# Attention's calls recorded and issued in one written order for all engines

## The chip, the cores and the metric

The kernel runs on one core of one Trainium2 chip. What is measured is the device time of one execution in microseconds (us). A core has five engines that each work off a list of their own: PE (matrix products and transposes), DVE and ACT (element-wise work and exponentials), POOL (element-wise work) and SP, which here only issues transfers. The lists meet at semaphores: an instruction waits until those that it needs have signalled.

## What is computed

Three stages follow each other. The first is causal attention with a decay over 32 heads (4 batches of 8), 576 positions and 64 columns a head:

```python
scores = scale * np.matmul(q, k.transpose(0, 1, 3, 2))
cum = np.cumsum(log_f, axis=-1)
decay = cum[:, :, :, None] - cum[:, :, None, :]
scores = np.where(causal, -1000000000.0, scores + decay)
scores = scores - np.max(scores, axis=-1, keepdims=True)
attn = np.exp(scores)
attn = attn / (np.sum(attn, axis=-1, keepdims=True) + 1e-09)
return np.matmul(attn, v).astype(np.float32)
```

Its result, 4 x 576 x 512, goes through the second stage: the real part of a Fourier transform over positions and columns is added, rows are normalized, and a layer 512 -> 2048 -> 512 with a ReLU is added. The third stage forms `x*cos(theta)` and `x*sin(theta)`, mixes positions with two 576 x 576 matrices, and adds a layer of 512 x 512.

## The kernel before, in words

Attention and the Fourier transforms of the first three batches are written in `phase1`. Heads go in 16 pairs (pair p has heads 2p and 2p+1); four pairs make a batch. A loop runs over heads, n from -1 to 32. In one turn it interleaves, step by step, the work of several heads, each written as a generator:

- `prep_units`: for head n+2, ACT casts the raw queries and keys to `hi` and `q` (L222, L224), and POOL forms the low parts, in `hi` and `kl` (L226, L228; DVE has one of them for head 0).
- `score_units`: for head n+1, five row blocks of 576, 448, 320, 192 and 66 columns. Each is two products, L247 (`hi` with `hi`) and L248 (`kl` with `q`), into a PSUM bank `pa` out of three. DVE adds the mask, takes the row minimum `mn` and writes `P` (L256); ACT exponentiates `P` in place, with row sums (L261). The block of 576 columns comes in two parts, 448 and 128. At the end of a pair ACT and DVE form `rz`, the reciprocal of the sums, and POOL spreads it to `wide` (L267).
- `turn_units`: for head n, the blocks of `P` are transposed (L286) into four banks `pb` out of three buffers, and copied to `PT` (L289), three by DVE, the fourth by ACT.
- `av_units`: for the pair before, 14 value products (L321) of `PT` with `v` into the bank `pt`, in 64-column halves of the two heads; then `spread` transposes `wide` (L300), one block into `pa`, four into `pb`, and ACT copies both to `R` (L301, 128 and 448 columns).
- `evac_pair`: DVE multiplies `pt` by `R` to `X` or `Y` (L347). For every second pair a few rows of `Y` are moved by transfers that SP issues (L356 to L363), and POOL forms `E` = X+Y and `O` = X-Y (L367, L370).
- `fft_units`: after four pairs, one batch's transform: POOL has `ee`, `oo` and the low parts `el`, `ol`, ACT `eh`, `oh`, PE the products L428, L439 and L451, and DVE and POOL what lies between (`yl`, `zl`, `ea`, `oa`, `u`).

Each engine's list is put together by a scheduler that goes by priorities: score products have 20 more than the rest, value products 100 more. In `av_units` the first value product also depends, by hand, on all eight copies to `PT` of its pair (the reason is named "one run"), so that none of the 14 comes before them. Phases 2 and 3 (normalization, layers, decoding of the 64-bit weights by DVE and ACT) stand behind; their work begins to be mixed in from turn n = 31 on, and the normalization of batch 0 from turn 29 on.

## Time and profile before

| | us |
|---|---|
| median of 3 runs | 939.33 |
| lowest and highest run | 938.42, 941.68 |
| profiled execution, its own time | 940.95 |
| its span in the trace | 939.2 |
| first matmul of attention starts | 9.44 |
| last block of value products starts | 249.42 |

The rows further below come from one profiled execution. A time is in us from the start of the span; a line number such as L321 is that of the code above. PE's matmuls overlap, since the engine takes the next before the last has left it: a busy PE is not a PE at its peak. PEld is PE's loading of weights (the stationary matrix), which goes beside its products. PEclk is the clock that PE was granted, as a share of the full one. A row that ends in `[0.36 <-DVE PT L289]` says that the engine stood idle for 0.36 us ahead of it, until DVE's instruction of L289 on tile `PT` had finished. An fp32 product has two records, so a block of 14 shows as x28.

### The profile page before, as it was taken

How to read it: one execution, taken by the hardware profiler on the slowest of the kernel's cores; microseconds unless marked ns; L12 is line 12 of the kernel's file. 1: busy time of each engine (PE TensorE's matmuls, PEld its weight loads, DVE VectorE, ACT ScalarE, POOL GpSimd, SP SyncE). 2: the span in 40 equal slices, each digit the busy share in tenths (PEclk: the TensorE clock that was granted, in tenths of full speed). 3: DMA queues.
4: the chain of work that ended last, by engine and by line, in shares of the span. 5: the costliest groups of instructions: out<-in, count | busy, mean ns of one | idle time of the engine just before them, and what ended most of it. 6: DMA issues, size and time to landing. Idle time of an engine off the chain costs nothing.

```text
span 939.2 us, 15860 instructions
## 1 busy us (share of the span) xinstructions
PE 894.1 (95%) x5960; PEld 841.5 (90%) x5960; DVE 606.7 (65%) x1495; ACT 417.8 (44%) x1014; POOL 326.3 (35%) x369
## 2 busy tenths in 40 slices
PE   4998999989788999999999999999999999999998
PEld 3777878777577999999999999999999999999998
DVE  8676676674899943456654565536687756747563
ACT  6888678685544332222221232223235534434331
POOL 6676788676601343000000000000035635425330
PEclk9999999999979999999999999999999999999999
DMA  5643423231233300013322122514310000010001
GB/s 167 202 149 106 130 93 114 83 105 40 82 97 93 90 1 1 1 46 90 91 91 90 45 90 74 199 29 127 109 51 2 1 26 27 14 40 1 26 27 51
DMA packets 23725, 68.04 MB, mean 72 GB/s; under 512 B 2906, under 2 KB 6362, under 8 KB 23648
## 3 DMA queue, kind: packets, MB, share of 16 engines
q1 hardware_dynamic: 20608, 62.88, 21.2%
q0 software_dynamic: 2320, 2.97, 1.2%
q10 hardware_dynamic: 720, 1.18, 0.4%
q8 instruction: 47, 0.77, 0.3%
q14 instruction: 30, 0.25, 0.1%
HBM read 57.91 MB, written 9.07 MB: 71 GB/s over the span
## 4 chain that ended last, share of the span: by engine, by line
PE 62%; DVE 5%; ACT 1%; issue 1%; DMA 0%; POOL 0%; DVEq 0%; SPq 0%; ACTq 0%
PE pa L767 19%; PE pb L781 11%; PE po L781 8%; PE pb L988 7%; PE pa L999 5%; PE pa L952 5%; PE po L988 5%; PE pa L948 1%; DVE u L789 1%; DVE kra L959 1%; DVE a L587 0%; DVE a L585 0%; DVE uc L754 0%; DVE kra L962 0%; PE pb L952 0%
## 5 line engine op out<-in xcount | busy, mean ns | idle before, releaser
L767 PE MATMUL pa<-un,wf 128*128 128x384 f32 x1152 | 221.4, 342 | 6.3 <-ACT un L755 3.4
L767 PEld LDWEIGHTS pa<-un,wf 128*128 128x128 f32 x1152 | 204.6, 191 | 10.2 <-DVE un L756 4.5
L773 DVE SCALAR_TENSOR_TENSOR h<-pa,h 128x384 fp32r<-128x384 f32 x96 | 52.4, 555 | 139.0 <-ACT h L772 139.0
L781 PE MATMUL pb<-h,wf 128*128 128x384 f32 x660 | 134.2, 337 | 0.3 <-DVE u L789 0.3
L781 PEld LDWEIGHTS pb<-h,wf 128*128 128x128 f32 x660 | 116.0, 188 | 1.1 <-DVE u L789 0.6
L781 PE MATMUL po<-h,wf 128*128 128x384 f32 x492 | 105.2, 340 | 0.4 <-ACT h L772 0.2
L772 ACT ACTIVATE h<-pa 128x384 fp32r<-128x384 f32 x96 | 45.7, 489 | 132.7 <-PE pa L767 130.0
L261 ACT ACTIVATE P<-P,mn 128x448 f32<-128x448 f32 (+4 forms) x160 | 89.0, 558 | 33.6 <-DVE mn L256 33.4
L988 PE MATMUL pb<-wtk,z 128*128 128x288 f32 x513 | 98.3, 295 | 1.3 <-ACT z L977 1.3
L944 POOL COPY xd<-u 128x64 f32<-128x64 f32 x32 | 6.9, 255 | 264.5 <-DVE u L789 254.5
L256 DVE CUSTOM_DVE_ANT_0 P<-pa,mask 128x448 f32<-128x448 f32 (+3 forms) x160 | 69.4, 457 | 42.1 <-PE pa L248 35.6
L781 PEld LDWEIGHTS po<-h,wf 128*128 128x128 f32 x492 | 86.2, 188 | 3.6 <-ACT h L772 1.9
L978 POOL TENSOR_TENSOR z<-kra,z 128x256 fp32r<-128x256 f32 x72 | 53.1, 752 | 93.5 <-ACT z L977 93.4
L247 PE MATMUL pa<-hi 128*128 128x448 f32 (+1 forms) x192 | 65.8, 364 | 20.5 <-DVE hi L226 9.4
L988 PEld LDWEIGHTS pb<-wtk,z 128*128 128x128 f32 x513 | 79.3, 188 | 2.0 <-ACT z L977 2.0
L988 PE MATMUL po<-wtk,z 128*128 128x288 f32 x351 | 75.2, 295 | 0.8 <-ACT z L977 0.8
L286 PE MATMUL pb<-ident,P 128*128 128x128 f32 (+2 forms) x480 | 73.9, 284 | 1.7 <-DVE uc L724 0.9
L247 PEld LDWEIGHTS pa<-hi 128*128 128x128 f32 x192 | 38.2, 204 | 30.1 <-issue 14.5
L289 DVE COPY PT<-pb 128x448 f32<-128x448 f32 (+1 forms) x96 | 55.6, 594 | 14.2 <-PE pb L286 13.3
L952 PE MATMUL pa<-wf,xs 128*128 128x256 f32 x456 | 64.1, 289 | 0.0
L286 PEld LDWEIGHTS pb<-ident,P 128*128 128x128 f32 (+2 forms) x480 | 56.6, 147 | 7.5 <-ACT P L261 1.2
L248 PE MATMUL pa<-kl,q 66*128 66x448 f32 (+1 forms) x192 | 58.0, 337 | 1.4 <-POOL kl L228 0.7
(206 smaller groups left out, 1667.0 us busy)
## 6 DMA issues: line engine op xcount, KB each, us to landing
raw<-in_qk SPq DMA_DIRECT2D x31, 576.0 KB
raw<-in_wf SPq DMA_DIRECT2D x32, 512.0 KB
raw<-in_wtk SPq DMA_DIRECT2D x18, 288.0 KB
v<-in_vp SPq DMA_DIRECT2D x16, 320.0 KB
out<-ob SPq DMA_DIRECT2D x12, 288.0 KB
dft<-in_dft POOLq DMA_DIRECT2D x8, 346.0 KB, 5.4
raw<-in_wth SPq DMA_DIRECT2D x4, 512.0 KB
st_wth<-raw SPq DMA_DIRECT2D x4, 512.0 KB
```

What stands on the lines that cost most here:

```text
L247: nc.tensor.matmul(t[:, 0 : b - a], hi[:, 1, q], hi[:, 0, a:b], start=True, stop=False)
L248: nc.tensor.matmul(t[:, 0 : b - a], q2[:, q], kl[:, g, a:b], start=False, stop=True)
L256: nc.vector.tensor_tensor_reduce(out=p[:, a:b], in0=t[:, 0 : b - a], in1=self.mask[:, m0 + a : m0 + b], scale=-0.125, scalar=least, op0=AL ...
L261: nc.scalar.activation(p, p, AF.Exp, bias=lowest, scale=-1.0, accum_out=zs[:, g, i : i + 1])
L286: nc.tensor.transpose(ps[:, o : o + n], src, self.ident[0:n, 0:n])
L289: copy = nc.scalar.copy(dst, ps[:, d : d + w]) if bank > 2 else nc.vector.tensor_copy(dst, ps[:, d : d + w])
L767: nc.tensor.matmul(ps[:, 0:CH], t[:, l, 128 * d : 128 * d + 128], un[r][:, d], start=n == 0, stop=n == 11)
L773: nc.vector.scalar_tensor_tensor(h[:, 1], ps[:, 0:CH], 0.0, f(h[:, 0]), ALU.max, ALU.subtract)
L781: nc.tensor.matmul(outs[d], t[:, l, 128 * d : 128 * d + 128], h[:, r], start=k % G == 0 and n == 0, stop=k % G == G - 1 and n == 2,)
L952: nc.tensor.matmul(th, xs[:, l, d], self.wth[d][:, r, 256 * hf : 256 * hf + 256], start=n == 0, stop=n == 11)
L978: nc.gpsimd.tensor_tensor(z[:, 1], t, f(z[:, 0]), ALU.subtract)
L988: nc.tensor.matmul(acc[k][th], z[:, l, 128 * k : 128 * k + 128], self.wtk[kt][:, r, 288 * th : 288 * th + 288], start=first and i == 0 and ...
```

## The change

Calls that `phase1` makes on the engines until turn n = 31 are no longer issued where they are written. `Recorder` takes the place of `nc` and keeps them in a list; early in turn n = 31 `emit` issues them, in the order that `order(0, n)` decodes from a table of digits. Each character of the table says which of the calls not yet issued comes next. They go out under `manual_schedule`, so that the order of issue is the order on every engine, and the buffers of PSUM follow each other in that order. What is written behind that point (the transposes of head 31, pair 15, phases 2 and 3) is scheduled as before. The dependency "one run" and the list of copies that it used are gone. Since recorded calls are issued from one place, they all bear line L71 in the lists of after.

```diff
--- before.py
+++ after.py
@@ -56,6 +56,33 @@
 
 def f(ap):
     return ap.bitcast(F32)
+
+
+class Recorder:
+    def __init__(self, nc):
+        self.nc, self.calls, self.live = nc, [], True
+
+    def __getattr__(self, name):
+        return Queue(self, name)
+
+    def emit(self, order):
+        for k in order:
+            engine, name, a, kw = self.calls[k]
+            getattr(getattr(self.nc, engine), name)(*a, **kw)
+        self.live = False
+
+
+class Queue:
+    def __init__(self, rec, engine):
+        self.rec, self.engine = rec, engine
+
+    def __getattr__(self, name):
+        def call(*a, **kw):
+            if not self.rec.live:
+                return getattr(getattr(self.rec.nc, self.engine), name)(*a, **kw)
+            self.rec.calls.append((self.engine, name, a, kw))
+
+        return call
 
 
 class Net:
@@ -274,7 +301,7 @@
         nc = self.nc
         P = hd["P"]
         PT = self.w3.tile([128, 1600], F32, tag="PT", name="PT", bufs=4)
-        hd["PT"], hd["copies"] = PT, []
+        hd["PT"] = PT
         for bank, pieces in enumerate(TURNED):
             ps = self.bank_b()
             for j, a, b, off in pieces:
@@ -286,8 +313,7 @@
                     nc.tensor.transpose(ps[:, o : o + n], src, self.ident[0:n, 0:n])
             d, w = TSKIP[bank], TWIDE[bank]
             dst = PT[:, PTOFF[bank] : PTOFF[bank] + w]
-            copy = nc.scalar.copy(dst, ps[:, d : d + w]) if bank > 2 else nc.vector.tensor_copy(dst, ps[:, d : d + w])
-            hd["copies"].append(copy)
+            (nc.scalar.copy if bank > 2 else nc.vector.tensor_copy)(dst, ps[:, d : d + w])
             yield
 
     def spread(self, p, T, wide):
@@ -310,7 +336,6 @@
             for j, a, b, off in pieces
         }
         yield
-        first = True
         with self.tc.high_priority(100):
             for j in range(5):
                 for lo_q, hi_q in ((0, SPLIT), (SPLIT, 576)):
@@ -318,21 +343,13 @@
                     if a >= hi_q:
                         continue
                     for g in (1, 0):
-                        ins = nc.tensor.matmul(
+                        nc.tensor.matmul(
                             T[64 * g : 64 * g + 64, T0 + a : T0 + hi_q],
                             v[:, j, g, :],
                             hds[g]["PT"][:, place[j, a] : place[j, a] + hi_q - a],
                             start=j == 0,
                             stop=j == 4 or (j == 1 and hi_q == SPLIT),
                         )
-                        if first:
-                            for copy in hds[0]["copies"] + hds[1]["copies"]:
-                                self.tc.add_manual_dep(
-                                    ins.ins, copy.ins.name,
-                                    mybir.DependencyInfo(mybir.DependencyClass.NoSync, mybir.DependencyReason.DATA),
-                                    reason="one run",
-                                )
-                            first = False
         for _ in range(5):
             yield
         R = self.spread(m % NP, T, wide)
@@ -478,6 +495,7 @@
     def phase1(self):
         pair, heads = self.p1_open()
         NH = B * H
+        rec = self.nc = Recorder(self.nc)
         pairs, heads, raws = {0: pair}, dict(enumerate(heads)), {}
         fft = None
         self.tick = 0
@@ -521,6 +539,9 @@
                 av = self.av_units(m, [heads[2 * m], heads[2 * m + 1]], T, pairs[m]["rz"], done)
             t = self.turn_units(heads[n]) if 0 <= n < NH else iter(())
             if n == NH - 1:
+                with self.tc.manual_schedule():
+                    rec.emit(order(0, len(rec.calls)))
+                self.nc = rec.nc
                 self.p1a.close()
                 self.p2_open()
                 self.load(0)
@@ -1099,6 +1120,47 @@
         self.pu0.close()
 
 
+DIGITS = "#$%&()*+,-./0123456789:;<=>?@ABCDEFGHIJKLMNOPQRSTUVWXYZ[]^_`abcdefghijklmnopqrstuvwxyz|"
+ORDERS = (
+    (
+        "&~$6~+X~,e~,e~,e~,e#*35=2)297*+1%)~$$).&|+%/.#$+##///#)-%+(*#)#**#$3<-=[#-811$.T5%;0..252~*p~*p.3361"
...
+    ),
+)
+
+
+def order(part, n):
+    left, taken, digits = list(range(n)), [], iter(ORDERS[part])
+    for c in digits:
+        k = DIGITS.find(c)
+        if k < 0:
+            k = DIGITS.index(next(digits)) * len(DIGITS) + DIGITS.index(next(digits))
+        taken.append(left.pop(k))
+    return taken
+
+
 def body(tc, ins, out):
     with ExitStack() as ctx:
         net = Net(ctx, tc, ins, out)
```

How instructions move shows at three places. First PE at the value products of pair 1 (heads 2 and 3; `P_107` is the buffer of head 4, whose work goes beside it). A row is a group of equal instructions, with the tile written, the tiles read, and the size. Before:

```order
L321 MATMUL pt<-PT,v 64x64 x2
L321 MATMUL pt<-PT,v 64x384 x2
L247 MATMUL pa<-hi 128x192
L248 MATMUL pa<-kl,q_100 128x192
L247 MATMUL pa<-hi 128x66
L248 MATMUL pa<-kl,q_100 128x66
L286 MATMUL pb<-ident,P_107 128x128 x2
L286 MATMUL pb<-ident,P_107 128x66
L286 MATMUL pb<-ident,P_107 128x126
L321 MATMUL pt<-PT,v 64x320 x2
L321 MATMUL pt<-PT,v 64x192 x2
L321 MATMUL pt<-PT,v 64x64 x2
```

After:

```order
L71 MATMUL pb<-ident,P_107 128x128
L71 MATMUL pt<-PT,v 64x192 x2
L71 MATMUL pt<-PT,v 64x384 x2
L71 MATMUL pt<-PT,v 64x64 x2
L71 MATMUL pt<-PT,v 64x384 x2
L71 MATMUL pt<-PT,v 64x320 x2
L71 MATMUL pt<-PT,v 64x192 x2
L71 MATMUL pt<-PT,v 64x64 x2
L71 MATMUL pa<-ident,wide 128x128
L71 MATMUL pb<-ident,P_107 128x128 x3
```

The last six of the 14 products stood behind two row blocks of scores and four transposes of head 4's third bank; now the 14 are one run, the transpose of `wide` into `pa` follows at once, and more of head 4's transposes stand behind.

Second, ACT around the same pair (`P_107` is head 4, `P_108` head 5). Before:

```order
L261 ACTIVATE P_108,zs_95<-P_108,mn 128x448
L261 ACTIVATE P_108,zs_95<-P_108,mn 128x576
L261 ACTIVATE P_108,zs_95<-P_108,mn 128x320
L222 CAST hi<-raw 128x1152
L224 CAST q_100<-raw 64x576
L261 ACTIVATE P_108,zs_95<-P_108,mn 128x192
L261 ACTIVATE P_108,zs_95<-P_108,mn 128x66
L289 COPY PT<-pb 128x320
L301 COPY R<-pa 128x128
```

After:

```order
L71 COPY PT<-pb 128x320
L71 ACTIVATE P_107,zs_95<-P_107,mn 128x448
L71 ACTIVATE P_107,zs_95<-P_107,mn 128x320
L71 CAST q_99<-raw 64x576
L71 ACTIVATE P_107,zs_95<-P_107,mn 128x192
L71 ACTIVATE P_107,zs_95<-P_107,mn 128x66
L71 COPY R<-pa 128x128
L71 ACTIVATE P_108,zs_95<-P_108,mn 128x576
L71 CAST hi<-raw 128x1152
```

The copy of 128 columns from `pa` to `R` stood behind all exponentials of head 5 and behind head 4's fourth copy to `PT`; it now stands between the last exponential of head 4 and the first of head 5, and the cast to `hi` follows directly on that first one.

Third, POOL in the third batch (`hi_2731` before and `hi_767` after are head 29; `hi_2836` and `hi_792` are head 30; `E`, `O`, `ee`, `oo`, `el` and `ol` belong to the batch's transform). Before:

```order
L391 MEMSET xx_3312 1x2
L367 TENSOR_TENSOR E_1940<-X_2358,Y_2555 128x576
L370 TENSOR_TENSOR O_1941<-X_2358,Y_2555 128x576
L226 TENSOR_TENSOR hi_2731<-raw_2596,hi_2731 64x576
L228 TENSOR_TENSOR kl_2514<-raw_2596,hi_2731 64x576
L399 TENSOR_TENSOR ee_2646<-E_1940 128x2x287
L267 TENSOR_SCALAR wide_2694<-rz1_98 128x640
L403 TENSOR_TENSOR oo_2647<-O_1941 128x2x287
L226 TENSOR_TENSOR hi_2836<-raw_2702,hi_2836 64x576
L228 TENSOR_TENSOR kl_2698<-raw_2702,hi_2836 64x576
```

After:

```order
L71 TENSOR_TENSOR hi_767<-raw_733,hi_767 64x576
L71 TENSOR_TENSOR xl_90<-xx_745,xh_89 1x290
L71 TENSOR_TENSOR kl_712<-raw_733,hi_767 64x576
L408 MEMSET xx_3315 1x2
L71 TENSOR_TENSOR E_596<-X_684,Y_725 128x576
L71 TENSOR_TENSOR ee_743<-E_596 128x2x287
L71 TENSOR_TENSOR O_597<-X_684,Y_725 128x576
L71 TENSOR_TENSOR oo_744<-O_597 128x2x287
L71 TENSOR_TENSOR el_747<-ee_743,eh_746 128x580
L71 TENSOR_TENSOR ol_749<-oo_744,oh_748 128x576
L71 TENSOR_SCALAR wide_755<-rz1_98 128x640
L71 TENSOR_TENSOR hi_792<-raw_758,hi_792 64x576
```

Head 29's `hi` and `kl` stood behind `E` and `O`; they now stand ahead of both, and `ee`, `oo`, `el` and `ol` stand ahead of `wide` and of head 30.

## Rows read from the trace of the kernel before

**Rows 1.** The chain of work that ended last, by engine, whole span

```profile
PE 62%; DVE 5%; ACT 1%; issue 1%; DMA 0%; POOL 0%; DVEq 0%; SPq 0%; ACTq 0%
```

**Rows 2.** Stretches: length, busy us of each engine (count), PEclk, DMA share, GB/s

```profile
41.00:52.00 11.00, 11.00 (x95) 9.03 (x93) 8.45 (x30) 10.50 (x30) 8.36 (x9) 1.00 0.91 267
145.70:149.20 3.50, 3.50 (x16) 3.42 (x17) 2.35 (x10) 3.17 (x14) 3.42 (x4) 0.51 0.00 0
210.00:214.00 4.00, 3.79 (x17) 1.85 (x19) 0.34 (x4) 1.94 (x7) 3.92 (x5) 0.58 0.29 81
33.00:255.00 222.00, 204.00 (x1591) 165.88 (x1589) 152.57 (x531) 165.51 (x465) 161.97 (x150) 0.98 0.34 105
255.00:320.00 65.00, 57.09 (x307) 51.39 (x308) 62.47 (x123) 28.97 (x56) 14.19 (x12) 0.84 0.32 94
```

**Rows 3.** What PE waited for, 33 to 255 us: total, times, longest

```profile
PE pa L247 <- POOL hi L226: 3.5, 2, 2.6
PE pa L247 <- DVE mn L256: 3.2, 8, 0.8
PE pt L321 <- DVE PT L289: 3.2, 5, 1.3
PE pa L247 <- ACT R L301: 1.1, 2, 0.7
...
PE pb L428 <- POOL el L406: 0.6, 2, 0.4
```

**Rows 4.** PE's timeline, value products: start, us, operation, records, idle time before

```profile
46.01 1.95 PE L321 MATMUL pt<-PT,v 128*64 128x192 f32 x16
...
48.90 1.20 PE L321 MATMUL pt<-PT,v 128*64 128x320 f32 x12
...
67.41 2.93 PE L321 MATMUL pt<-PT,v 128*64 128x192 f32 x28
...
89.74 1.95 PE L321 MATMUL pt<-PT,v 128*64 128x192 f32 x16 [1.34 <-DVE PT L289]
...
249.42 2.93 PE L321 MATMUL pt<-PT,v 128*64 128x192 f32 x28 [0.36 <-DVE PT L289]
```

**Rows 5.** POOL's timeline ahead of head 29's cast

```profile
205.89 1.42 POOL L367 TENSOR_TENSOR E<-X,Y 128x576 f32<-128x576 f32 x1 [2.15 <-DVE PT L289]
...
208.75 1.40 POOL L226 TENSOR_TENSOR hi<-raw,hi 64x576 fp32r<-64x576 f32 x1
```

**Rows 6.** PE's timeline at head 29's first score product

```profile
210.21 0.47 PE L247 MATMUL pa<-hi 128*128 128x448 f32 x1 [2.58 <-POOL hi L226]
210.60 4.59 PE L321 MATMUL pt<-PT,v 128*64 128x192 f32 x28
```

**Rows 7.** ACT's timeline in one pair without FFT work

```profile
41.93 0.67 ACT L261 ACTIVATE P<-P,mn 128x448 f32<-128x448 f32 x1
...
42.60 0.55 ACT L261 ACTIVATE P<-P,mn 128x320 f32<-128x320 f32 x1
...
43.56 0.45 ACT L261 ACTIVATE P<-P,mn 128x192 f32<-128x192 f32 x1
...
45.05 0.67 ACT L224 CAST q<-raw 64x576 fp32r<-64x576 f32 x1
45.62 0.35 ACT L261 ACTIVATE P<-P,mn 128x66 f32<-128x66 f32 x1
...
45.97 0.40 ACT L289 COPY PT<-pb 128x320 f32<-128x320 f32 x1
```

**Rows 8.** What ACT waited for, 33 to 255 us

```profile
ACT P L261 <- DVE mn L256: 27.2, 28, 2.9
ACT R L301 <- PE pb L300: 4.8, 5, 2.9
```

**Rows 9.** What POOL waited for, 33 to 255 us

```profile
POOL Y L358 <- DMA Y<-Y: 12.2, 3, 6.0
```

**Rows 10.** DVE's copies to PT at the start

```profile
22.09 1.14 DVE L289 COPY PT<-pb 128x448 f32<-128x448 f32 x2
```

23 lines of the change are left out of this document (added).

## The prediction

> **What bounds the kernel now.** The profiled execution spans 939.20 us and took 940.95 us, so 1.75 us lie around its span; the median of the runs shown is 939.33 us. Sums below are made against 940.95, and the last step takes off 1.6 us to stand against the median.
>
> I read the chain of the work that ended last first. Its shares are those of phases 2 and 3 [rows 1], which the edit does not reorder. So attention counts only through the moment at which it ends. The table by stages says the same: from 255 to 320 us DVE is busy 62.5 of 65 us [rows 2], with decoding, norm and the rest of the FFT, all issued behind the recorded part. That stretch begins when attention ends (pair 15's value products start at 249.42 us [rows 4]), so I let a microsecond won or lost before 250 us pass to the end unchanged.
>
> Between 33 and 255 us the same table shows PE busy 204 of 222 us, ACT 165.5, POOL 162, DVE 152.6: no engine is full over the whole stretch. Inside it there are two regimes. Pairs without FFT work (37 to 90 us) go by ACT: from 41 to 52 us ACT is busy 10.50 of 11 us [rows 2], and from pair 1's value products to pair 5's it is 89.74 - 46.01 = 43.7 us [rows 4], 10.9 for each of four pairs. Pairs with FFT work (90 to 240 us) go by whichever engine comes last, and there PE's table of waits has nearly all its entries [rows 3].
>
> [...] From 41 to 52 us the matmul row reads 11.00 and the weight row 9.03 [rows 2]; by the first nothing is to be won there, by the second up to 2 us in 11, some 10 us over five pairs, and the sum below would come out near 922. My sum takes nothing there because of ACT's row.
>
> **The change, part by part.** The number and kind of compute instructions stay. What changes is their order on each engine, and with it which wait comes last.
>
> *Value products in one block.* Before, 9 of 16 pairs have their 14 products in two groups (25 groups of L321 stand in PE's timeline). The two groups take 1.95 + 1.20 = 3.15 us, a whole one 2.93 [rows 4]: 0.22 us a split, 9 x 0.22 = 2.0 us. Five of the nine lie before 92 us, where ACT sets the pace, and I count them at nothing: if ACT did not cover them, they would give 1.1 us more. Four count: **-0.9**.
>
> *The wait at the block's head.* Before, PE stands 3.2 us ahead of L321 for PT's copies by DVE [rows 3]. The written order puts each recorded block behind transposes and scores of the next head, so the copy has that long to land. Pair 15's block is left with the scheduler, and it keeps its 0.36 us [rows 4]. The ends are 0 (the time reappears at the next wait) and -2.8 (all but that); I take **-2.0**, nearer to the far end since work stands in between, less part of the 1.34 us at 89.74 [rows 4], which ACT may fill.
>
> *Head 29's cast.* At 205.89 us POOL starts E after a wait of 2.15 us, then O, and only then, at 208.75, hi of head 29 [rows 5]. PE idles 2.58 us for it until 210.21 [rows 6]. [...] In the written order head 29's hi and kl stand ahead of E, ee and O, and head 30's hi behind them is wanted only after a run of FFT matmuls. So **-2.6** for the wait, and **-1.6** for the block at full clock (4.59 - 2.93, rounded down). If some other engine is late in the same place, both are 0; that is a rival.
>
> *R's transposes.* The single transpose into `pa` now stands right behind the block, and the four into `pb` later. PE's wait for ACT's R, 1.1 us twice over [rows 3], is a score matmul that wants the `pa` bank back; with R copied earlier I count **-1.1**, ends 0 and -1.1. The price is on ACT. Its R copy of 128 columns stands in a fixed place, behind the exps of one head and ahead of those of the next, and waits until PE has finished the block. Take pair 1. PE's last step ahead of the block is a transpose into the bank that ACT's copy of PT empties. From the start of that copy: copy 0.4, transposes and handover 0.4, the block 2.93, R's transpose 0.3: 4.0 us. ACT's own work in that time: the copy 0.40, exps of 448, 320, 192 and 66 columns 0.67, 0.55, 0.45, 0.35, the q cast 0.67 [rows 7], 3.1 in all. ACT idles some 0.9 us. Before, that pair gives ACT idle time too (0.5 of 11 us by [rows 2]), so in ACT-paced pairs the new period is 10.5 + 0.9 less what fits elsewhere, 10.6 to 11.2 against 10.9. Over five pairs that is -1.5 to +1.5: **0**. In pairs with FFT work ACT has idle time in plenty (its waits for `mn` alone are 27.2 us [rows 8]), which hides 0.9 us.
>
> *FFT's low parts.* PE waits 0.6 us for POOL's el now [rows 3]. In the written order the first matmul on el follows the first ones on eh at once, with POOL's el still to come: **+0.4**, ends 0 and +2 (in the three batches that are recorded with heads, about 0.7 each). E waits for the moved rows of Y, 12.2 us of POOL's waits in three batches [rows 9]; behind E on POOL stand wide, hi and kl of the next heads. The order puts hi and kl of a head ahead of E in two batches, so I count no change; its bad end is in the second rival.
>
> *The start.* DVE now copies head 0's first turned bank ahead of head 1's reductions. A copy takes about 0.57 us [rows 10]; head 1's exps and all behind them come that much later: **+0.7**, ends 0 and +1.1 (one or two copies).
>
> *The second fall of the clock*, granted 0.51 from 145.7 to 149.2 us [rows 2], may stay or go. At about half the rate 3.5 us do the work of 1.8, so it is worth 0 to -1.7; I take 0, since nothing in the order bears on it plainly. Waits for `mn` (3.2 us [rows 3]) follow ACT and DVE; I leave them.
>
> Sum: -0.9 - 2.0 - 2.6 - 1.6 - 1.1 + 0.4 + 0.7 = -7.1. 940.95 - 7.1 = 933.85, less 1.6 is **932.2 us**.
>
> **Rivals.** *ACT's R copy holds every pair (slower).* ACT works its list strictly in order, so the exps behind R wait for the block, and with them the transposes and the next block. Speaking for it: before, ACT's waits for R come to only 4.8 us, 5 times, the longest 2.9 [rows 8], because the copy came when it was ready. Speaking against it: from 33 to 255 us ACT is idle 56 us. Price: 0.9 to 1.0 us in 15 pairs, 15 us, less the 4.8 it waits now, is +10.2; with the other terms but R's (-0.9 - 2.0 - 2.6 - 1.6 + 0.4 + 0.7 = -6.0), +4.2, so 940.95 + 4.2 - 1.6 = **943.5**. It decides if ACT's wait for R is over 9 us in all and pairs with FFT pay it too. [...]
>
> *The waits change place (no difference).* Head 29's wait goes, but blocks and splits are hidden by ACT or come back elsewhere (0 in place of -0.9, -2.0 and -1.1), and el costs its +2, because E stands on POOL until Y's rows have landed. -4.2 + 2.0 + 0.7 = -1.5: **937.8**. For it: ACT's 10.50 of 11; against it: pairs with FFT work wait for POOL and DVE, not ACT.
>
> *Nearly all waits go (much faster).* The waits in [rows 3] come to 11.6 us, and 15.4 with the eight smaller rows of that table; with the splits 2.0, head 29's block 1.6 and the second fall of the clock 1.7, less 1.1 for start and el: -19.6, **919.8**. For it: an order written with the whole chain in view can cover them all. Against it: 3.2 of them are for `mn`, which comes from the chain of DVE and ACT, and ACT-paced pairs cannot shrink below 10.5.
>
> *The change does not act as described* (blocks parted by waits inside them): the order of the program shows 14 products in a row and only the load of v to wait for, so 2 in 100; it would leave the time within 0.3%.
>
> **How the numbers follow.** Chances: the forecast 0.42, much faster 0.16, places change 0.18, ACT's R 0.22, not as described 0.02. About 0.3% (2.8 us) is what a measurement of this kernel can tell from no change, so the limits are 936.5 and 942.1. Faster: 0.42 + 0.16 = 0.58; same: 0.18 + 0.02 = 0.20; slower 0.22. The range goes from 919 (below it, less than 0.1) to 946 (the slow rival with the far ends of start and el, +0.4 and +1.6): what is left out is about 0.15.
>
> **What would show it.** In the profile of the changed kernel: 16 groups of value products of about 2.9 us; no wait of PE for POOL's hi near 210 us, and granted clock 1.00 there; PE's waits for PT ahead of the blocks under 1 us in all; ACT's wait for R between 5 and 9 us, most of it before 92 us; pair 15's block at about 242 us, not 249.4, and everything behind it moved by the same amount. I am wrong if ACT's wait for R is 12 us or more, if POOL's E stands longer for Y with hi behind it, or if the stretch after 255 us does not move with attention's end.

## The result

| | median of runs, us (lowest to highest) | profiled execution | its span | pair 15's block starts |
|---|---|---|---|---|
| before | 940.50 (938.42 to 941.81) | 940.95 | 939.2 | 249.4 |
| after | 928.53 (927.10 to 930.36) | 927.50 | 925.7 | 233.2 |

The ratio is 0.9876, with an interval of 0.9846 to 0.9906: the change makes the kernel about 12 us faster. The forecast was 932.2, 919 to 946. From profile to profile the span is 13.5 us shorter. Attention ends 16.2 us earlier, and the rest of the kernel takes 2.7 us longer (925.7 - 233.2 = 692.5 against 689.8).

To place the 16.2 us I compare both kernels at equal matrix work: the time at which the same sum of products has been issued on PE, each product counted by its usual distance to the next one. After is 1.5 us ahead when the first pair's value products come (at 33 us), 0.5 us ahead at 91 us, and 16.2 us ahead at pair 15's block. So the start gained 1.5, the pairs without FFT work lost 1.0, and the pairs with FFT work gained 15.7. The cut at 91 us is good to about 1 us, since the two orders place the same products differently there: at 96 us the lead reads 1.4. The table of stretches shows these two regimes, first before, then after (columns as in [rows 2]):

```profile
33.00:91.80 58.80, 55.48 (x448) 43.58 (x446) 43.21 (x161) 52.28 (x153) 42.23 (x36) 1.00 0.47 147
91.80:249.40 157.60, 144.84 (x1110) 119.81 (x1110) 104.46 (x360) 109.01 (x307) 118.55 (x112) 0.98 0.29 90
```

```profile
33.00:91.30 58.30, 55.38 (x433) 42.85 (x433) 40.05 (x154) 51.92 (x150) 42.78 (x36) 1.00 0.47 148
91.30:233.20 141.90, 138.23 (x1117) 117.62 (x1115) 104.58 (x363) 111.77 (x317) 118.06 (x112) 1.00 0.31 101
210.00:214.00 4.00, 4.00 (x33) 3.92 (x31) 2.19 (x6) 1.12 (x3) 2.46 (x2) 1.00 0.00 0
145.00:150.00 5.00, 4.26 (x35) 3.06 (x37) 3.44 (x12) 5.00 (x15) 4.08 (x4) 1.00 0.02 5
```

In the second stretch PE was idle for 157.6 - 144.84 = 12.8 us and is now idle for 3.7: 9.1 us less. Its busy time for the same work fell from 144.84 to 138.23: 6.6 us less. Of that, 3.4 us are the two falls of the clock (0.51 and 0.58 in [rows 2], 1.00 now): 3.5 us x 0.49 + 4 us x 0.42. Four splits make 0.6: from a group's start to that of the product behind it the two groups of pair 1 take 1.88 and 1.13 us and a whole block 2.86, so a split costs 0.15 and not the 0.22 of the durations in [rows 4], which overlap the next product. Some 2.6 us of busy time are left. An estimate: the last product ahead of a wait has nothing to overlap it. A lone transpose takes 0.33 us and seven in a row 0.94 (in after, at 199.96 and 196.64 us), so each further one adds 0.10; with 21 waits in the table before and 9 after, 12 x 0.23 = 2.8. No run tests this.

Of the 9.1 us of idle time 8.3 stand in the tables of waits. What PE waited for in the second stretch, before (parts) and after (all of it; us in total, times, longest):

```profile
PE pa L247 <- POOL hi L226: 3.5, 2, 2.6
PE pa L247 <- DVE mn L256: 1.8, 5, 0.7
...
PE pt L321 <- DVE PT L289: 1.1, 2, 0.8
...
PE pb L300 <- DVE PT L289: 0.7, 1, 0.7
...
PE pb L451 <- ACT PT L289: 0.5, 1, 0.5
...
PE pb L286 <- DVE PT L289: 0.2, 1, 0.2
```

```profile
PE pb L71 <- ACT PT L71: 1.3, 2, 0.7
PE pb L71 <- DVE PT L71: 0.8, 2, 0.6
PE pt L346 <- DVE PT L316: 0.5, 1, 0.5
PE pb L313 <- ACT PT L71: 0.4, 1, 0.4
PE pb L71 <- ACT P L71: 0.2, 1, 0.2
PE pb L71 <- DVE u L71: 0.2, 1, 0.2
PE pt L71 <- DVE X L71: 0.2, 1, 0.2
```

POOL's `hi` and `kl` (4.2 us), `mn` (1.8) and ACT's `R` (1.3) are gone as releasers. Waits for `PT` are not: 2.5 us before (the four rows shown), 3.0 after. They moved from the blocks (`pt`) to transposes into `pb`. The other rows went from 2.1 (`uc`, `yl`, `el`, `X`) to 0.6 (`P`, `u`, `X`).

Value products now come in 16 whole groups. PE's timeline of after, at pair 1 and at pair 13:

```profile
44.65 2.93 PE L71 MATMUL pt<-PT,v 128*64 128x192 f32 x28
...
202.86 2.93 PE L71 MATMUL pt<-PT,v 128*64 128x192 f32 x28 [0.16 <-DVE X L71]
```

Pair 13's block took 4.59 us [rows 6], with a granted clock of 0.58 from 210 to 214 us [rows 2], and takes 2.93 now. POOL's timeline of after at the place of [rows 5]:

```profile
191.94 1.41 POOL L71 TENSOR_TENSOR hi<-raw,hi 64x576 fp32r<-64x576 f32 x1
...
194.18 1.42 POOL L71 TENSOR_TENSOR kl<-raw,hi 64x576 fp32r<-64x576 f32 x1
...
196.43 1.42 POOL L71 TENSOR_TENSOR E<-X,Y 128x576 f32<-128x576 f32 x1 [0.80 <-DVE mn L71]
```

`hi` and `kl` of head 29 fill time that POOL would stand idle ahead of `E`: without them (a_hi29 below) it waits 3.05 us there. And what ACT waited for from 33 to 255 us, after, against [rows 8]:

```profile
ACT R L71 <- PE pa L71: 5.7, 7, 1.3
...
ACT R L71 <- PE pb L71: 3.7, 2, 2.5
...
ACT R L71 <- DVE Y L71: 1.9, 2, 1.0
```

ACT's waits for `R` sum to 11.3 us; 4.1 of them, five times, lie before 94 us, in the pairs without FFT work.

### The profile page after: what moved, and what is told of

It reads as the page before. It is cut to its first block, busy times and chain, and to the rows that moved or that the text cites. A ratio compares the mean times of both kernels' runs of the same rounds, so it can differ in the third digit from the quotient of the medians.

```text
span 925.7 us, 15855 instructions
## 1 busy us (share of the span) xinstructions
PE 888.4 (96%) x5960; PEld 839.1 (91%) x5960; DVE 604.6 (65%) x1495; ACT 417.7 (45%) x1014; POOL 329.5 (36%) x369
## 4 chain that ended last, share of the span: by engine, by line
PE 58%; DVE 9%; ACT 2%; issue 1%; DMA 0%; POOL 0%; ACTq 0%; DVEq 0%; SPq 0%
PE pa L788 19%; PE pb L802 11%; PE po L802 8%; PE pa L1020 5%; PE pb L1009 5%; PE pa L973 4%; PE po L1009 3%; DVE kra L980 1%; DVE kra L983 1%; DVE kra L982 1%; DVE kra L981 1%; DVE kra L997 1%; DVE kra L979 1%; DVE u L810 1%; PE pa L969 1%
## 5 line engine op out<-in xcount | busy, mean ns | idle before, releaser
L71 ACT ACTIVATE P<-P,mn 128x576 f32<-128x576 f32 (+4 forms) x155 | 86.4, 559 | 16.3 <-DVE mn L71 16.2
L71 PE MATMUL pb<-ident,P 128*128 128x128 f32 (+2 forms) x465 | 81.8, 285 | 4.5 <-DVE PT L71 2.3
L71 DVE CUSTOM_DVE_ANT_0 P<-pa,mask 128x448 f32<-128x448 f32 (+3 forms) x155 | 66.3, 454 | 20.3 <-PE pa L71 17.1
L71 PE MATMUL pa<-hi 128*128 128x448 f32 (+1 forms) x186 | 65.4, 367 | 1.0 <-DVE mn L283 0.5
L71 PEld LDWEIGHTS pb<-ident,P 128*128 128x128 f32 (+2 forms) x465 | 56.0, 145 | 11.1 <-DVE PT L71 3.9
L71 DVE COPY PT<-pb 128x448 f32<-128x448 f32 (+1 forms) x93 | 52.9, 594 | 11.7 <-PE pb L71 10.5
L1009 PEld LDWEIGHTS po<-wtk,z 128*128 128x128 f32 x351 | 57.3, 188 | 1.2 <-ACT z L998 1.2
L973 PEld LDWEIGHTS pa<-wf,xs 128*128 128x128 f32 x456 | 57.1, 190 | 0.0
```

Source lines behind the costliest of these rows:

```text
L71: getattr(getattr(self.nc, engine), name)(*a, **kw)
L973: nc.tensor.matmul(th, xs[:, l, d], self.wth[d][:, r, 256 * hf : 256 * hf + 256], start=n == 0, stop=n == 11)
L1009: nc.tensor.matmul(acc[k][th], z[:, l, 128 * k : 128 * k + 128], self.wtk[kt][:, r, 288 * th : 288 * th + 288], start=first and i == 0 and ...
```

## The experiments

Ratios are against runs of the kernel before on the same chip (their medians were 939.58 to 940.74). All variants but the kernel before keep the recorder and differ from after in the table of the order alone, so the edits are shown as rows of an engine's list (- without the edit, + with it). "Block 15" is the start of pair 15's value products in the profile, the end of attention; "rest" is the span less that. Both come from one profiled execution of each kernel, while the runs of one kernel lie up to 5.3 us apart (e_Rhi), so a difference of a microsecond or two in these columns is no finding by itself. Where I say "at equal work", products are counted as above.

| kernel | median, us (runs) | ratio to before, interval | block 15 | rest |
|---|---|---|---|---|
| before | 940.50 (4) | 1 | 249.4 | 689.8 |
| after | 928.53 (4) | 0.9876, 0.9846 to 0.9906 | 233.2 | 692.5 |
| e_before | 941.16 (11) | 1.0011, 1.0002 to 1.0020 | 249.1 | 690.1 |
| e_join | 943.90 (6) | 1.0041, 1.0026 to 1.0056 | 251.3 | 689.3 |
| e_hi29 | 941.47 (11) | 1.0013, 1.0004 to 1.0021 | 248.0 | 691.8 |
| a_hi29 | 934.31 (6) | 0.9944, 0.9928 to 0.9960 | 240.9 | 691.3 |
| e_R | 946.66 (6) | 1.0057, 1.0038 to 1.0076 | 249.6 | 696.5 |
| e_Rhi | 945.41 (11) | 1.0052, 1.0038 to 1.0065 | 250.2 | 691.9 |
| a_split | 936.29 (6) | 0.9956, 0.9941 to 0.9972 | 245.1 | 689.4 |
| a_start | 929.16 (5) | 0.9884, 0.9866 to 0.9903 | 233.7 | 692.5 |
| h_ba | 928.14 (5) | 0.9876, 0.9856 to 0.9897 | 235.6 | 693.4 |
| h_ab | 945.59 (6) | 1.0058, 1.0044 to 1.0072 | 248.3 | 696.9 |
| a_Rlate | 926.58 (5) | 0.9855, 0.9839 to 0.9870 | 234.7 | 690.1 |
| a_av | 933.74 (6) | 0.9936, 0.9917 to 0.9956 | 235.0 | 696.6 |

**Is it the order at all?** In e_before the recorder stays, and its table gives the order of before.

```diff
 ORDERS = (
     (
-        "&~$6~+X~,e~,e~,e~,e#*35=2)297*+1%)~$$).&|+%/.#$+##///#)-%+(*#)#**#$3<-=[#-811$.T5%;0..252~*p~*p.3361"
+        "~$7~+Y~,f~,f~,f~,f&#3%;++++335>~$(~$)~+N~+N+#$$$$((((++++.%-**(nn%//$#$..5#&&&$##33$7@%*$//#66#-45~$7~"
...
```

> The changed kernel's recording and issuing is kept, but the table holds the order of the kernel before for every engine. Theory A (the order is the whole gain): the time is that of the kernel before, 940 us within 2 us, and pair 15's value products start at 249.4 us within 1 us. Rival B (the recording itself, with finer waits and banks handed out by order of issue, brings part of the 12 us): 3 us or more faster than before, 937 us or less, without any change of order.

It took 0.1% more than before (1.0002 to 1.0020), with block 15 at 249.1 us. Recording and issuing from one place give nothing; everything is the order.

**Whole blocks alone.** e_join is before's order; in the nine parted pairs the first eight products move down to the other six. PE, pair 1:

```diff
 L71 MATMUL pa<-kl,q_100 128x448
-L71 MATMUL pt<-PT,v 64x192 x2
-L71 MATMUL pt<-PT,v 64x384 x2
-L71 MATMUL pt<-PT,v 64x64 x2
-L71 MATMUL pt<-PT,v 64x384 x2
 L71 MATMUL pa<-hi 128x320
...
 L71 MATMUL pb<-ident,P_107 128x126
+L71 MATMUL pt<-PT,v 64x192 x2
+L71 MATMUL pt<-PT,v 64x384 x2
+L71 MATMUL pt<-PT,v 64x64 x2
+L71 MATMUL pt<-PT,v 64x384 x2
 L71 MATMUL pt<-PT,v 64x320 x2
```

> Order of the kernel before, with one part of the change: in the nine split pairs the first eight value products are moved down to stand directly ahead of the last six, so that all blocks are whole. Theory A (whole blocks are worth 0.22 us each, and five of nine lie where ACT sets the pace): 0 to 2 us faster than before, some 939 us. Rival B (one block is what brings the gain): 6 us or more faster, 934 us or less. Rival C (the block comes later, so DVE's evacuation and the banks come late): 2 us or more slower.

Measured: 0.4% slower than before, 3.4 us, as Rival C had it. What PE waited for in e_join, 33 to 252 us:

```profile
PE pa L71 <- DVE mn L71: 5.0, 14, 0.7
PE pa L71 <- POOL hi L71: 4.0, 3, 2.2
PE pa L71 <- POOL kl L71: 1.3, 3, 0.7
...
PE pt L71 <- DVE PT L71: 1.1, 2, 0.8
```

The blocks wait 1.7 us less for `PT` than in [rows 3] (1.1 and pair 15's 0.4 against 3.2), as hoped. But the score products behind them now come to PE earlier than `mn` (5.0 against 3.2 us), `hi` and `kl` (5.3 against 4.2), and the nine saved changes are lost in that. The clock adds to it: behind a wait of 0.85 us for `el` at 219 us the granted clock reads 0.57 from 218 to 226 us, where e_before has 1.00. At equal work e_join is 1.5 us ahead of e_before at 216 us and 2.2 behind at 228, and so it ends. Whole blocks are no gain by themselves.

**Head 29's cast alone.** e_hi29 is before's order with one edit on POOL:

```diff
-L71 TENSOR_TENSOR E<-X,Y 128x576
-L71 TENSOR_TENSOR O<-X,Y 128x576
 L71 TENSOR_TENSOR hi<-raw,hi 64x576
 L71 TENSOR_TENSOR kl<-raw,hi 64x576
+L71 TENSOR_TENSOR E<-X,Y 128x576
+L71 TENSOR_TENSOR O<-X,Y 128x576
```

> Order of the kernel before, with one part of the change: on POOL the low parts of head 29 (hi, kl) stand ahead of E of the third batch instead of behind O. Theory A: PE's wait of 2.58 us at 210 us goes, and with it the fall of the granted clock behind it (1.66 us in pair 13's block): 4.2 us faster than before, about 936 us, pair 14's block at 234.3 instead of 238.5. Rival B: E, ee and el come 2.8 us later instead, and PE waits for them: 0 to 1 us faster.

Measured: no difference from e_before. PE no longer waits for `hi`, and waits as long for something else. PE, DVE and POOL in e_hi29:

```profile
209.44 4.31 PE L71 MATMUL pt<-PT,v 128*64 128x192 f32 x28 [2.91 <-DVE PT L71]
```

```profile
208.16 0.76 DVE L71 TENSOR_TENSOR X<-pt,R 128x576 f32<-128x576 f32 x1 [1.82 <-POOL O L71]
208.84 0.55 DVE L71 COPY PT<-pb 128x384 f32<-128x384 f32 x1
```

```profile
205.35 1.41 POOL L71 TENSOR_TENSOR E<-X,Y 128x576 f32<-128x576 f32 x1
206.73 1.40 POOL L71 TENSOR_TENSOR O<-X,Y 128x576 f32<-128x576 f32 x1
```

`E` and `O` read the pair before's `X`, so DVE can't write the next `X` until POOL has done `O`. The copy to `PT` that the value products want stands behind that `X` on DVE. With the cast out of the way, the chain `O`, `X`, `PT` takes its place: 2.91 us instead of 2.58 [rows 6], with the block at 4.31 us behind it. That chain was just as late in the kernel before. DVE there:

```profile
208.71 0.76 DVE L347 TENSOR_TENSOR X<-pt,R 128x576 f32<-128x576 f32 x1 [0.99 <-POOL O L370]
209.38 0.55 DVE L289 COPY PT<-pb 128x384 f32<-128x384 f32 x1
```

It ended at 209.93 us, 0.2 us ahead of `hi` (208.75 + 1.40 [rows 5]). The 1.1 us by which block 15 comes earlier than in e_before are not the edit's: POOL's list first differs at 202 us, and there e_hi29 already stood 0.9 us ahead at equal work.

**The same two casts put back in the new order.** a_hi29 is after, with the two behind `O` on POOL:

```diff
-L71 TENSOR_TENSOR hi<-raw,hi 64x576
 L71 TENSOR_TENSOR xl<-xx,xh 1x290
-L71 TENSOR_TENSOR kl<-raw,hi 64x576
...
 L71 TENSOR_TENSOR O<-X,Y 128x576
+L71 TENSOR_TENSOR hi<-raw,hi 64x576
+L71 TENSOR_TENSOR kl<-raw,hi 64x576
```

> Order of the changed kernel, with one part undone: on POOL the low parts of head 29 stand behind E, ee and O of the third batch. Theory A (this order on POOL alone is worth 4.2 us): PE waits 2 to 4 us for hi near 200 us, the granted clock falls behind it, 932 to 933 us. Rival B (PE's written order has other work to hide it): the changed kernel's 928.5 us within 1.5 us.

Measured: 5.8 us slower than after, block 15 7.7 us later. PE's timeline, and the stretch behind it:

```profile
202.69 0.74 PE L71 MATMUL pa<-hi 128*128 128x448 f32 x1 [4.86 <-POOL hi L71]
204.16 0.74 PE L71 MATMUL pa<-kl,q 66*128 66x448 f32 x1 [0.73 <-POOL kl L71]
```

```profile
203.00:211.00 8.00, 7.05 (x34) 5.88 (x35) 4.49 (x13) 3.79 (x8) 5.91 (x5) 0.62 0.23 75
```

5.6 us of waiting, and 8 x 0.38 = 3.0 us of clock. The same edit is worth nothing in the old order and 5.8 us in the new one. The lists show a reason why the chain of `O`, `X` and `PT` doesn't step in here: after's PE has head 29's first score product 5.5 us ahead of pair 13's block (197.34 and 202.86 us), before's 0.4 us (210.21 and 210.60 [rows 6]), so in after the copy to `PT` is wanted much later than `hi`. No run moved that block alone.

**R and Y earlier.** In after, pairs 7 and 11 (the last of a batch) have R's transposes ahead of the block, so that `Y` and the moves of its rows follow the block at once; before, `Y` came 5.5 and 7.3 us behind the block. e_R does only this to before's order, with ACT's copies and the moves on SP along. PE, pair 7:

```diff
+L71 MATMUL pb<-ident,wide 128x66
+L71 MATMUL pb<-ident,wide 128x126
+L71 MATMUL pb<-ident,wide 128x128 x2
+L71 MATMUL pa<-ident,wide 128x128
 L71 MATMUL pt<-PT,v 64x192 x2
...
-L71 MATMUL pa<-ident,wide 128x128
...
-L71 MATMUL pb<-ident,wide 128x66
-L71 MATMUL pb<-ident,wide 128x126
-L71 MATMUL pb<-ident,wide 128x128 x2
```

> Order of the kernel before; for the last pair of the second and third batch (pairs 7 and 11) R's five transposes stand ahead of the block, ACT's two copies of R beside it, and DVE's Y with SP's three moves behind its end, 5.1 and 7.0 us earlier than before. Theory D (the chain from a block by R, Y, the moves, E and O to the next X sets the pace in batches with FFT work): E and O of these batches start some 5 us earlier, PE's waits near 145 and 210 us (0.77 + 0.87 and 2.75 us) and the falls of the granted clock behind them shrink: 4 to 7 us faster than the replayed order of before (941.2 us), 934 to 937. Rival E (a late E costs nothing by itself; the waits are filled by other late work): 940 us or more.

Measured: block 15 at 249.6 us, where e_before has 249.1. At the place of the edit Theory D came true: `E` of the third batch starts without a wait (2.33 us in e_before), PE waits 0.30 us for `hi` where e_before has 2.77, and pair 13's block takes 2.93 us. (POOL's three waits to write `Y`, 11.9 us in e_before, stand at other places and stay at 12.0.) But the next wait was close behind. PE in e_R:

```profile
209.55 0.47 PE L71 MATMUL pa<-hi 128*128 128x448 f32 x1 [0.30 <-POOL hi L71]
...
218.82 0.58 PE L71 MATMUL pb<-dft,el 128*128 128x258 f32 x1 [0.85 <-POOL el L71]
```

From 218 to 222 us the granted clock reads 0.59 there, 1.00 in e_before. At equal work e_R gains 3.5 us on e_before from 204 to 216 us and gives 1.9 back by 222; it had lost 1.2 between 180 and 204. Since it stood 1.0 us behind ahead of its first edited place, the edit is worth 0.6 at block 15. The whole is 5.5 us slower, all of it in the rest.

e_Rhi joins both edits, since POOL, freed from waiting for `Y`, could do the cast and `E` in time. PE's rows at one of the pairs, then POOL's:

```diff
+L71 MATMUL pa<-ident,wide 128x128
 L71 MATMUL pt<-PT,v 64x192 x2
...
+L71 TENSOR_TENSOR hi<-raw,hi 64x576
+L71 TENSOR_TENSOR kl<-raw,hi 64x576
 L71 TENSOR_TENSOR E<-X,Y 128x576
```

> As the kernel with R, Y and the moves early for pairs 7 and 11 in the order of before, and in addition POOL's hi and kl of head 29 ahead of E. Theory D: with X no longer held by O, the early hi now pays as well, so the wait at 210 us is gone: 1 to 3 us faster than that kernel, some 933 to 936 us, no granted clock under 0.9 between 205 and 215 us. Rival E: no difference between the two.

Measured: block 15 at 250.2, no gain. POOL's and DVE's timelines in e_Rhi:

```profile
206.08 1.42 POOL L71 TENSOR_TENSOR E<-X,Y 128x576 f32<-128x576 f32 x1
```

```profile
208.89 0.76 DVE L71 TENSOR_TENSOR X<-pt,R 128x576 f32<-128x576 f32 x1 [1.79 <-POOL O L71]
```

`E` starts without a wait and still late: POOL is busy 15.6 of the 16.7 us from 190.8 to 207.5, and the same chain through `O` and `X` holds PE for 2.87 us. So the cast ahead of `E` brings back the wait that e_R had removed. The list ahead of `E` is too long; after has the two casts at 191.94 and 194.18, in time that POOL had spent waiting.

**Blocks parted in the new order.** In a_split each of after's 15 recorded blocks is parted 8 + 6, with four products or transposes of other work (beside `R`'s) between. PE, pair 0:

```diff
 L71 MATMUL pt<-PT,v 64x384 x2
+L71 MATMUL pa<-ident,wide 128x128
+L71 MATMUL pb<-ident,P_107 128x126
+L71 MATMUL pb<-ident,P_107 128x128 x2
+L71 MATMUL pa<-hi 128x66
 L71 MATMUL pt<-PT,v 64x320 x2
```

> Order of the changed kernel, but each of its 15 recorded blocks is parted: the last six value products stand behind the next four matmuls or transposes (R's not counted). Theory A (a split costs PE 0.22 us at its two ends, as read from the durations, and nothing where ACT sets the pace): 1 to 3 us slower than the changed kernel, 929.5 to 931.5. Rival B (one block is what brings the gain): 6 us or more slower, 934.5 or more. Rival F (PE has room, a split is free): within 1 us of 928.5.

Measured: 7.8 us slower than after, block 15 11.9 us later. The splits themselves are 15 x 0.15 = 2.3 us. The rest came as waits (10.6 us in PE's table up to block 15, 6.2 in after) and as clock:

```profile
44.22 0.36 PE L71 MATMUL pb<-ident,P 128*128 128x128 f32 x1 [0.93 <-ACT PT L71]
44.51 3.55 PE L71 MATMUL pt<-PT,v 128*64 128x192 f32 x16
```

```profile
33.00:60.00 27.00, 25.39 (x184) 17.93 (x182) 16.76 (x61) 21.95 (x66) 16.89 (x15) 0.94 0.57 172
60.00:96.00 36.00, 33.09 (x246) 26.16 (x243) 23.73 (x89) 30.03 (x83) 26.12 (x22) 0.95 0.37 113
150.00:160.00 10.00, 8.11 (x55) 5.44 (x53) 4.19 (x16) 6.58 (x18) 8.93 (x8) 0.83 0.02 9
```

Eight products took 3.55 us, with a granted clock of 0.57 from 44 to 48 us; in before they take 1.95 [rows 4] at 1.00 [rows 2]. The three stretches lose 27 x 0.06 + 36 x 0.05 + 10 x 0.17 = 5.1 us. So in the new order a split costs 0.8 us (11.9 / 15), also in the pairs without FFT work, where I had counted it at nothing: 4.2 us are lost by 96 us. This is more than the change undone, since before parted nine blocks and a_split parts 15.

**The start.** a_start has before's order up to 24 us and after's behind. PE:

```diff
-L71 MATMUL pb<-ident,P_107 128x128 x7
-L71 MATMUL pa<-hi 128x448
-L71 MATMUL pa<-hi 128x128
 L71 MATMUL pa<-hi 128x448
 L71 MATMUL pa<-kl,q_100 128x448
+L71 MATMUL pa<-hi 128x128
```

> Order of the changed kernel, but the calls that the kernel before issues until 24 us stand in the order of before (head 0's transposes behind head 1's scores on PE, DVE's first copy behind head 1's reductions). My prediction had the new start 0.7 us slower: then this kernel is 0.7 us faster, 927.8. The trace of the changed kernel has it 1.2 us ahead at the same amount of work: then this one is 1 to 1.5 us slower, 929.5 to 930, if ACT, which sets the pace until 92 us, does not take the gain back; if it does, there is no difference at pair 5.

Measured: 0.6 us slower than after, which these runs can't tell from nothing.

**Which half?** h_ba has before's order up to 85 us and after's from there; h_ab the reverse. The place of the change of order in h_ba, PE, against before's order:

```diff
 L71 MATMUL pb<-ident,wide 128x66
+L71 MATMUL pa<-hi 128x128
+L71 MATMUL pa<-kl,q_99 128x128
 L71 MATMUL pb<-ident,wide 128x126
+L71 MATMUL pa<-hi 128x448
+L71 MATMUL pa<-kl,q_99 128x448
 L71 MATMUL pb<-ident,wide 128x128 x2
```

> The 693 calls that the kernel before issues until 85 us (start and pairs without FFT work) in its order, all others in the order of the changed kernel. Theory G (the whole gain lies in the pairs with FFT work): 927 to 930 us, the changed kernel's time within 1.5 us, and pair 15's block at 233 to 235 us. Rival H (the order ahead of 85 us is needed for the gain behind it): 933 us or more.

> The 695 calls that the changed kernel issues until 85 us in its order, all others in the order of the kernel before. Theory G: no gain is left, 940 to 942 us, and pair 15's block at 249 to 250 us. Rival H: 937 us or less.

h_ba has the whole gain in its runs (0.9876). In its profile block 15 comes 2.4 us later than in after, but that is lost by 96 us: from there on h_ba stays 2.4 to 2.7 us behind after at equal work. h_ab has none at the end of attention (0.8 us against e_before), and loses 6.8 us in the rest. So the new order pays in the pairs with FFT work alone.

**ACT's R copy.** In a_Rlate ACT's copy of 128 columns stands two calls later in pairs 0 to 4, where ACT had waited for it:

```diff
 L71 ACTIVATE P_107,zs_95<-P_107,mn 128x66
-L71 COPY R<-pa 128x128
 L71 ACTIVATE P_108,zs_95<-P_108,mn 128x576
 L71 CAST hi<-raw 128x1152
+L71 COPY R<-pa 128x128
```

> Order of the changed kernel, but ACT's copy of 128 columns to R stands two calls later in pairs 0 to 4, behind two more exponentials or casts. My prediction gave R's fixed place a price of 0.9 us of idle ACT in each pair that ACT paces. The trace of the changed kernel shows 4.1 us of ACT waiting for R between 33 and 94 us, 5 times. Theory I (ACT sets the pace there and the wait is its only loss): 2 to 4 us earlier at pair 5, and 925 to 927 us if the rest passes it on. Rival J (the pa bank is held longer, score matmuls wait, or another engine comes last): within 1 us of 928.5.

ACT's waits from 33 to 94 us, in a_Rlate:

```profile
ACT R L71 <- PE pa L71: 1.2, 2, 1.0
```

and PE there:

```profile
73.50 0.44 PE L71 MATMUL pa<-hi 128*128 128x448 f32 x1 [1.03 <-DVE mn L71]
```

ACT's wait for `R` fell from 4.1 to 1.2 us, other waits came in its place, and block 15 stands 1.5 us later than in after. At equal work a_Rlate is within 0.5 us of after up to 66 us and 1.8 behind at 72 us; no wait of PE for `mn` in after is longer than 0.2 us there. So taking ACT's wait for `R` away in this manner gained the end of attention nothing. The total is the best of all kernels, 926.58, its interval overlapping after's. It lies in Theory I's range, but not by Theory I's way: pair 5 comes no earlier, and what is won lies in the rest (690.1 against 692.5), which the edit doesn't touch by its own lines.

**The place of the blocks of pairs 7 and 11.** a_av moves these two blocks up to ahead of `R`'s transposes:

```diff
 L71 MATMUL pb<-ident,P_107 128x126
+L71 MATMUL pt<-PT,v 64x192 x2
+L71 MATMUL pt<-PT,v 64x384 x2
...
 L71 MATMUL pa<-ident,wide 128x128
...
 L71 MATMUL pb<-ident,P_107 128x128 x3
-L71 MATMUL pt<-PT,v 64x192 x2
-L71 MATMUL pt<-PT,v 64x384 x2
```

> Order of the changed kernel, but PE's blocks of pairs 7 and 11, which stand some 9 us behind the last copy to PT that they need (at 130.6 and 185.4 us), stand directly ahead of R's transposes of their pair (at 121.7 and 176.8 us). Nothing else moves, so DVE's Y comes no earlier. Theory K (a late block is what PE works on while the exponentials and copies of the next heads come; put early it leaves a gap in its old place): PE waits for PT, P or mn appear near 130 and 185 us, pair 15's block comes 2 to 5 us later, 235 to 238 us. Rival L (PE has work enough at both places): pair 15's block within 0.7 us of 233.5. The time follows by as much, apart from what the stretch behind attention adds or takes (rest of 689 to 693 us behind that block).

Measured: 5.2 us slower than after. Its start happened to be 1.4 us earlier; from there attention takes 3.2 us more, and the rest 4.1. PE's timeline in a_av at the first place, and the stretch around it in a_av and in after:

```profile
132.81 0.33 PE L71 MATMUL pa<-ident,wide 128*128 128x128 f32 x1 [0.85 <-POOL wide L71]
```

```profile
132.00:137.00 5.00, 3.93 (x31) 2.99 (x33) 4.51 (x16) 5.00 (x15) 4.73 (x6) 1.00 0.27 100
```

```profile
132.00:137.00 5.00, 5.00 (x49) 3.97 (x47) 3.66 (x12) 3.85 (x13) 2.97 (x4) 1.00 0.29 83
```

The second place reads alike (a wait of 0.84 us at 189.12, PE busy 3.92 of 5 us, 5.00 in after). The block of 2.93 us is work that PE can do while the others catch up. In after it lies directly ahead of these two places; moved away, it leaves PE idle for 1.1 us in each, while ACT is busy all 5 us and DVE 4.5 and 4.8.

## Why the prediction was right, and where it was not

The sign and the mechanism were right (waits of PE in pairs with FFT work go, attention ends earlier, and the kernel with it), and the time lies inside the range, 3.7 us below the forecast. The size was less right than that reads: the sum had 7.1 us, the medians show 12.0, and the forecast had been set against a median of three runs that is 1.2 us below that of all four. Of the marks named, 16 whole blocks, no wait for `hi` at 210 us, the clock of 1.00 there and under 1 us of waits at the blocks' heads (0.9) came. Two did not: block 15 was named at 242 us and came at 233.2, and ACT's wait for `R` was named at 5 to 9 us, most of it before 92 us, and came as 11.3, with 4.1 before 94 us. The terms of the sum were off in both directions, so that part of the agreement is luck. "Found" is an account by the rows of the profiles, not what single edits give:

| step | forecast | found |
|---|---|---|
| splits | -0.9 | -0.6 by rows in FFT pairs; a split undone costs 0.8 each (a_split) |
| waits for PT | -2.0 | -0.5 (blocks -2.3, transposes +1.8); in FFT pairs +0.5 |
| head 29, wait and clock | -4.2 | -2.6 and -1.7 |
| R on PE | -1.1 | -1.3 |
| el | +0.4 | -0.4 |
| start | +0.7 | -1.5 |
| second fall of the clock | 0 | -1.7 |
| pairs without FFT work | 0 | +1.0 |
| mn, in FFT pairs | 0 | -1.8 |
| kl, the other hi, uc, yl | 0 | -2.9 |
| PE's busy time without a row | 0 | about -2.6 |
| what follows attention | 0 | +2.7 |

With the value of the FFT pairs for PT, so that nothing of the other pairs counts twice, the last column sums to -12.9, of the 13.5 us that are there.

- *Waits for PT.* The step failed by its own far end: "the time reappears at the next wait" was one of the bounds, and it happened. At the blocks 3.2 us became 0.9, but transposes (`pb`) wait 3.2 us for copies to `PT` in after's table from 33 us to the end of attention, against 1.4 before. The value of -2.0 was too near the other end.
- *Head 29.* Place, size and the clock behind it were right: pair 13's block, the source of the -1.6, took 4.59 us [rows 6] at 0.58 [rows 2] and takes 2.93 at 1.00 (200 to 205 us in after). And a_hi29 shows that the new order needs the cast there. The reason given was incomplete: the cast ahead of `E` alone is worth nothing (e_hi29), since `O` then holds `X` and `X` holds `PT`. The forecast said that both terms are 0 "if some other engine is late in the same place"; in the old order that is what happens, by 0.2 us, and it is the rest of the order that prevents it. In the old order the wait also goes without the cast, when `Y` comes earlier (e_R).
- *R and ACT.* PE's side was right. On ACT's side the price was right: it waits for `R` 4.1 us in five pairs, 0.82 each where 0.9 was worked out. What stands behind the copy waited with it: in after ACT idles 1.20 us ahead of pair 1's copy at 47.88 us, and head 5's first exponential, whose `mn` was out at 44.08 (DVE, 44.00 + 0.08), starts at 48.04. These pairs became at most 1.0 us longer, inside the -1.5 to +1.5 given; a_Rlate, with 2.9 us less of that wait, made them no shorter. That pairs with FFT work would wait another 7.2 us was not foreseen. The slow rival's sign, over 9 us of such waits in all, came (11.3 us) without its second condition: pairs with FFT work did not pay.
- *Start.* Wrong sign. From 8 to 33 us PE's waits for `mn` fell from 2.9 to 1.1 us, one of 0.4 for `kl` went, and one of 1.6 us for a `PT` copy appeared: only the copy had been counted. One profile isn't enough for its size. At equal work (where the first block comes) the six kernels with the new start stand at 30.7 to 33.0 us, 31.9 in the mean, the eight with the old one at 32.9 to 34.5, 33.5 in the mean. Part of it is given back: at equal work a_start is 0.9 us behind after at 36 us and 0.5 from 90 us on, and its runs lose 0.6.
- *What was left at zero.* The second fall of the clock, `mn` in FFT pairs, and the smaller rows went too: 6.4 us by the table, which the "nearly all waits go" rival held. Whether the order took away the fall of the clock is not shown, since e_hi29 is without it in the old order (last section). What came is between that rival's 919.8 and the forecast, nearer to the forecast. The reason against that rival, that `mn` comes from the chain of DVE and ACT, did not hold: its 1.8 us are gone while DVE and ACT do the same work.
- *Attention's end is passed on unchanged.* Off by 2.7 us in the profiles. Block 15 came 16.2 us earlier, the end 13.5 (12.0 by the medians). In the 85 us from that block on PE is idle 11.7 us after (84.5 less 72.82 busy) and 9.8 before. The part behind is put together anew for each kernel, and its length went from 689.3 to 696.9 us among all variants, though none changes its code. Its order does change: of the 4370 PE instructions behind the recorded part, all stand in after's places in a_hi29, and 178 do not in h_ab. The differences arise at once: the same products are reached 80 to 88 us behind block 15, and from there all kernels take 604.4 to 606.2 us. The four longest (e_R, h_ba, h_ab, a_av; 693.4 to 696.9) have the lowest granted clock in the 90 us behind block 15, 0.85 to 0.87 against 0.89 to 0.91 in the others. That doesn't explain after (0.91) against before (0.89). What sets the length is not settled: ACT's wait for the raw weights is longer in after, which may be cause or result.

ACT's waits, after from 225 to 320 us, then before from 240 to 335 us:

```profile
ACT a L601 <- DMA raw<-in_wf: 19.1, 11, 3.1
```

```profile
ACT a L580 <- DMA raw<-in_wf: 14.2, 10, 3.0
```

By PE's weight row [rows 2] the prediction saw up to 10 us in the pairs without FFT work, by ACT's row nothing. ACT is busy 52.28 of 58.8 us there against 43.58 of the weight row, and nothing was won in that stretch (at most 1.0 us lost at equal work). In the pairs with FFT work the weight row went from 119.81 of 157.6 us to 117.62 of 141.9, so there it had room.

So the parts are no sum. Done alone in the old order, whole blocks, head 29 and R are worth -2.2, +1.1 and -0.5 us at block 15 against e_before (plus is earlier); less what stood there ahead of each edit's first place, -2.2, +0.2 and +0.6. Changed alone in the new order, splits, head 29 and the place of two blocks cost 11.9, 7.7 and 3.2, together more than the 16.2 that there are (a_split goes beyond undoing, as said). Where the traces were followed, a removed wait had another right behind it; of the orders tried, only the whole one for the pairs with FFT work moves the end.

## What to carry to other kernels

Where engines work lists in order, price a reordering by the second-latest chain at the same place, not by the wait that it removes: here POOL's cast hid a chain through `O`, `X` and `PT` that ended 0.2 us before it. A single move tried in the old order and found worthless says little about the same move inside a new order. And a gain at the end of one stage should be followed into the next: 2.7 of 16.2 us were given back there.

## What the runs showed of the hardware

- Short waits and long ones had different followers. Behind PE's waits of 2.58 us [rows 6], 2.91 us (e_hi29) and 4.86 us (a_hi29) the granted clock reads under 1.00 (0.58 from 210 to 214 us [rows 2], 0.79 from 206 to 214 us, and 0.62 from 203 to 211 us); around the single waits of 0.84 and 0.85 us in a_av it reads 1.00 (187 to 192 and 132 to 137 us). The length of the last wait alone doesn't tell: in a_split the clock reads 0.57 from 44 to 48 us, behind a wait of 0.93 us, while in before it reads 1.00 from 89 to 93 us, around the wait of 1.34 us at 89.74 [rows 4].
- The same order doesn't always give the same falls. Up to 200 us e_hi29 and e_before have the same lists, and both have PE waits of 0.61 and 0.7 us just ahead of 145.5 us. Then e_hi29 and, below it, e_before read:

```profile
145.00:149.00 4.00, 3.67 (x27) 3.19 (x27) 3.55 (x16) 4.00 (x17) 3.92 (x5) 1.00 0.00 0
```

```profile
145.00:149.00 4.00, 3.64 (x16) 3.56 (x17) 2.67 (x12) 3.57 (x16) 3.92 (x5) 0.57 0.00 0
```

- From 89 to 93 us it is the other way round: 0.57 in e_hi29 (a wait of 1.81 us) and 1.00 in e_before (1.63 us). So a fall behind waits of this size, or its absence, in a single profile is not yet the order's doing.
- The first pair's value products come at 32.0 to 33.9 us in after, a_hi29, a_split, a_av, a_Rlate and h_ab, though each engine's calls up to there are the same. So a difference of one or two microseconds between single profiles at this place says nothing about the order.
